# Key, query and value casts spread over three engines in a routed attention and gated FFN kernel, with a new order of all work

## The chip, the cores and the metric

The kernel runs on one core of one Trainium2 chip. The metric is device time in microseconds (us) of one execution. Three executions of the kernel before are shown; their median is 237.74 us.

## The reference, cut to what matters

Attention with 4 batches, 8 heads, 768 tokens and 64 values a head: each query and key is assigned to one of 16 centroids of its head, and a query attends only to keys of its own cluster. The result is the input of a feed-forward block with a short convolution as gate.

```python
q_assign = argmax(einsum('bhsd,hcd->bhsc', q_n, c_n))      # k_assign alike
mask = q_assign[..., :, None] == k_assign[..., None, :]
scores = where(mask, scale * q @ k.T, -1e9)
x = softmax(scores) @ v                                     # heads side by side: 512 columns
h = maximum(x @ w_in, 0)                                    # 512 -> 1024
conv_out = sum(conv_w[i] * shifted(h, i - 1) for i in 0..2) # along the sequence
out = (h * sigmoid(conv_out)) @ w_out                       # 1024 -> 512
```

## The kernel before, in words

**Pairs.** The 32 heads are worked in 16 pairs (0 to 15), four to a batch. A pair's queries and keys are loaded as f32, turned so that the head dimension lies on the partitions (tile `qkT`, 128 rows: head one on rows 0 to 63, head two on 64 to 127), and assigned to clusters. For the scores they are needed as f16 in a tile `ext` of 67 rows a head: 64 rows of values and three rows that carry the cluster number as a large negative bias. There are five `ext` tiles, used in turn (pair g has number g mod 5), and five f16 value tiles.

**Casts.** All casts end in `copy` (L317 to L321), which by a letter takes ScalarE (`a`, L319), VectorE (`d`, L321) or GpSimd (`p`, L321 as well). There are four ways to fill `ext`: `cast_by_head` (L327, token `CD`: 64 x 768, pair 0), `cast_half` (L334, `CE`: one head, queries or keys, half of the tokens, 64 x 384, straight to its place; eight of them to a pair), and `cast_pair` (L330, `CC`: both heads together, 128 x 384, four to a pair), after which head two lies on rows 64 to 127 and `shift_pair` (L338, `CX`) moves it to rows 0 to 63 of its own place by a DMA of 192 KB on SyncE's queue. `cast_v` (L342, `CV`) casts the values of one head, 128 x 384.

**Attention.** A batch has eight attention steps: per pair the first 512 queries, then the other 256. `scores` (L452, `S`) makes the score products into PSUM on TensorE, `exps` (L466, `E`) takes 1024 exponentials a row on ScalarE (144 such instructions), `values` (L476, `V`) multiplies with the values, `reciprocals` (L493, `P`) and `normalize` (L497, `N`) finish on VectorE.

**Assignment.** `assign` (L345, `A`) multiplies with the centroids, and seven steps of `argmax` (L373, `M0` to `M6`) find the cluster on VectorE, the last two on either VectorE or GpSimd.

**FFN.** Once a batch's attention is done its FFN runs between the attention steps of the next: `ffn_in` (L545, `I`), `relu` (L560, `Ra` on ScalarE or `Rd` on VectorE), `tap` (L590, tokens `a`, `b`, `c`) and `add_side` (L595, `s`, `u`) for the convolution on VectorE, `tanh` (L613, `H`, ScalarE), `gate` (L623, `G`, VectorE), `ffn_out` (L638, `O`), `evac` (L653, `Fd` or `Fa`) and the store. For the last units the convolution runs on TensorE with diagonal matrices (`conv`, L600, `W`), which the set-up makes from the weights (24 instructions, L779, `_tpd` on VectorE or `_tp` on GpSimd).

**Order.** Nothing reorders the program. A string `PLAN` (L26 on) of about 1,700 tokens is walked by L882, and each token issues one step. Each engine runs its own instructions in that order, and waits for the others by semaphores. The letter in a cast's token names its engine.

Of the kernel before, what the change touches and what calls it, by code (L numbers as in the profile page):

```python
# [26 lines left out]
    "_cent LQ.0.0 _hz.1 _zero _pk.2 _cT _k.0@0 _v.2 _n0 _pk.3 LK.0.0 _k.1@0 _id _k.2@0 _cw0 _v.0 _k.3@0 _io "  # L27
    "_id16 _pk.1 _k.4@0 LV.0 _n1 _k.5@0 _v.3 _hz.2 _pk.0 LK.0.1 _k.6@0 _nq _v.1 _v.4 _k.7@0 _hz.0 _n8 _n2 "
    "LQ.0.1 _k.8@0 _k.9@0 LQ.1.0 _k.10@0 _n3@1 _cw1@2 LK.1.0 _k.11@0 _n4 T.0.0@3 _n6 _n7 LK.1.1 T.0.1@0 _n5 "
    "_cw2 Qa.0.0 _tpd.0 _kk.0@1 _tp.1 _kk.1@2 Qd.0.1 LV.1 CVa.0.1 _kk.2@3 _kk.3@1 _kk.4@2 _tpd.2 CVa.0.0 "  # L30
    "A.0.0@0 _tpd.3 _tpd.4 LQ.1.1 CDa.0.0.0 _tpd.5 _kk.5@2 _tpd.6 _kk.6@1 CDp.0.0.1 M0.0.0 _kk.7@3 M1.0.0 "
    "T.0.2@3 M2.0.0 T.0.3@0 LV.2 Qa.0.2 M3.0.0 _tpd.7 M4.0.0 Qa.0.3 LQ.2.0 M5.0.0 M6.0.0 CDa.0.1.0 A.0.1@0 "
    "_tpd.8 _tpd.9 _tp.10 KB.0.0.1@3 M0.0.1 KB.0.0.0@1 CDp.0.1.1 BBa.0.0.1.0 M1.0.1 LK.2.0 T.1.2@0 "
    "BBd.0.0.0.0 BBd.0.0.0.1 S.0.0@0 M2.0.1 LQ.2.1 BBd.0.0.1.1 CVa.1.0 CVp.1.1 S.0.1@1 "
    "E.0.0@0 M3.0.1 LK.2.1 M4.0.1 T.1.0@3 M5.0.1 E.0.1@1 M6.0.1 T.1.1@1 LQ.3.0 _tp.11 Qd.1.0 S.0.2@0 Qd.1.2 "
    "LK.3.0 V.0.0@2 CVa.2.1 CEp.1.0.0.0 V.0.1@2 Qa.1.1 KB.0.1.0@3 CEd.1.0.1.1 KB.0.1.1@0 E.0.2@0 LQ.3.1 "
    "_tpd.12 CEp.1.1.1.0 BBd.0.1.0.1 A.1@1 BBd.0.1.0.0 CEp.1.1.1.1 BBd.0.1.1.0 LK.3.1 CEa.1.0.1.0 BBd.0.1.1.1 "
    "V.0.2@2 CEp.1.1.0.0 CEa.1.1.0.1 S.0.3@1 M0.1 LQ.4.0 CEa.1.0.0.1 S.0.4@0 M1.1 E.0.3@1 T.2.0@1 P.0.0 M2.1 "
    "T.2.1@0 _tpd.13 Qa.2.0 M3.1 T.2.2@3 E.0.4@0 M4.1 LQ.4.1 CEp.2.0.0.0 S.0.5@1 M5.1 CEp.2.1.0.0 V.0.3@1 "
    "Qd.2.2 Qa.2.1 LK.4.1 S.4.0@0 M6.1 _tpd.14 CEa.2.1.1.1 CEp.2.0.1.1 K.1@3 A.2@0 Ba.1 CEd.2.1.0.1 CVa.2.0 "  # L40
    "BX.1 N.0.0 T.3.0@3 E.0.5@1 CEp.2.0.0.1 M0.2 V.0.4@1 LQ.5.0 CEp.2.1.1.0 T.3.2@2 Qd.3.0 "
    "E.4.0@0 CEp.2.0.1.0 V.0.5@1 LQ.5.1 M1.2 T.3.1@0 CCp.3.0.0 P.0.1 LQ.6.0 S.4.1@1 Qa.3.2 N.0.1 S.4.2@0 M2.2 "
    "E.4.1@1 LK.4.0 X.0@2 Qd.3.1 CCp.3.1.1 V.4.0@1 T.4.0@3 E.4.2@0 M3.2 LK.5.1 A.3@0 CCp.3.1.0 M4.2 CCp.3.0.1 "
    "LK.5.0 Qa.4.0 M5.2 S.1.0@1 M6p.2 M0.3 Ya.0 S.1.1@0 CCp.4.0.0 M1.3 "
    "E.1.0@1 K.2@0 V.4.1@1 V.4.2@1 Bd.2 M2.3 BX.2 T.5.0@0 E.1.1@0 P.4.0 N.4.0 S.1.2@1 CX.3 _tp.15 Qd.5.0 "
    "V.1.0@1 E.1.2@1 S.1.3@0 LW.0 M3.3 CCp.5.0.0 V.1.1@1 M4.3 X.4@0 T.4.2@2 E.1.3@0 _tpd.16 M5p.3 LV.3 "
    "V.1.2@1 _tp.17 Qd.4.2 S.1.4@1 Ya.4 S.1.5@0 P.1.0 E.1.4@1 CCp.4.1.1 T.4.1@2 LV.4 N.1.0 T.5.2@0 M6p.3 "
    "E.1.5@0 Qd.4.1 S.2.0@1 Qd.5.2 K.3@1 T.5.1@3 CCp.4.0.1 "
    "E.2.0@1 S.2.1@0 Bd.3 _tpd.18 BX.3 _tpd.19 A.4@1 _tpd.20 _tpd.21 E.2.1@0 _tpd.22 _tpd.23 CCp.5.1.1 LW.1 "
    "S.2.2@1 M0.4 Qa.5.1 CCp.4.1.0 V.1.3@0 LW.2 S.2.3@0 M1.4 E.2.2@1 CCp.5.1.0 A.5@3 CWd.0 E.2.3@0 LW.3 "  # L50
    "S.2.4@1 M2.4 V.1.4@0 CVp.3.0 V.1.5@0 E.2.4@1 M0.5 S.2.5@0 CCp.5.0.1 LW.4 M1.5 V.2.0@1 CVp.4.0 E.2.5@0 "
    "V.2.1@1 P.1.1 V.2.2@1 M3.4 S.3.0@1 CVp.4.1 P.2.0 M4.4 V.2.3@3 LW.5 "
    "E.3.0@1 S.3.1@0 N.2.0 M2.5 V.2.4@3 V.2.5@3 E.3.1@0 N.1.1 S.3.2@1 M3.5 LW.6 P.2.1 M5p.4 V.3.0@0 M4.5 "
    "X.1@1 CWp.1 E.3.2@1 S.3.3@0 M5.5 Yd.1 V.3.1@0 E.3.3@0 M6.5 M6.4 S.3.4@1 N.2.1 CWp.2 V.3.2@0 K.5@3 "
    "E.3.4@1 X.2@1 LW.7 Bd.5 S.3.5@0 Yd.2 K.4@3 CVp.3.1 P.3.0 E.3.5@0 Bd.4 S.5.0@1 CWd.3 V.3.3@3 LQ.7.0 "
    "V.3.4@3 N.3.0 "
    "E.5.0@1 S.5.1@0 CWd.4 V.3.5@3 E.5.1@0 S.5.2@1 P.3.1 LQ.6.1 N.3.1 V.5.0@0 X.3@3 E.5.2@1 S.6.0@0 LK.6.1 "
    "Yd.3 V.5.1@0 I.0.1@3 "
    "E.6.0@0 LK.6.0 CWd.6 I.0.0@1 CWa.5 LQ.7.1 Rd.0.1 I.1.1@2 CX.4 Ra.0.0 CWa.7 b.0.0 I.1.0@1 LK.7.1 b.0.1 "
    "c.0.0 Ra.1.1 c.0.1 V.5.2@0 a.0.0 S.6.1@1 Ra.1.0 a.0.1 I.2.1@2 P.5.0 C.0 s.0 E.6.1@1 C.1 LZ.8.0.0 S.6.2@0 "  # L60
    "u.0 Ra.2.1 I.2.0@1 a.1.0 LZ.8.0.1 H.0 a.1.1 b.1.0 I.3.0@2 b.1.1 LZ.8.0.2 c.1.0 E.6.2@0 G.0 LK.7.0 "
    "T.6.0@3 S.7.0@1 Ra.2.0 BX.4 S.7.1@0 c.1.1 Qa.6.0 C.2 I.3.1@1 s.1 Ra.3.0 LZ.8.0.3 "
# [851 lines left out]
```

## Time and profile before

| | |
|---|---|
| median of three executions | 237.74 us (237.20 to 237.86) |
| profiled execution | 237.67 us, of it span 235.9 us, 1.8 us around it |
| granted TensorE clock | 1.00 throughout |
| TensorE, busy | 224.7 us (95%) |
| VectorE, busy | 217.1 us (92%), 565 instructions |
| ScalarE, busy | 207.5 us (88%), 273 instructions |
| GpSimd, busy | 72.3 us (31%), 166 instructions |
| DMA engines, share of the span | 65% in SyncE's queue |

Busy time counts from an instruction's start to its end, overlaps once. An instruction's end overlaps the start of the next on its engine by some 0.07 us, so the distance from start to start, which the timeline shows, is a bit less than the mean duration in the groups. A matmul's end is modelled, so that a busy TensorE may still have gaps. In the groups of instructions L321 holds VectorE's and GpSimd's copies and casts alike; the engine and the tile tell them apart.

### The profile page before, as it was taken

The page shows a single profiled execution, that of the slowest core. Times are in us where ns is not written, and L with a number is a line of the kernel's source. Part 1 is how long each engine was busy: PE and PEld are TensorE (multiplying, and loading weights), DVE is VectorE, ACT ScalarE, POOL GpSimd, SP SyncE. Part 2 cuts the span into 40 slices and gives each one's busy share as a digit, 9 for nine tenths or more (in the row PEclk, how much of TensorE's full clock was granted, in tenths as well). Part 3 has the DMA queues.
Part 4 walks back from the last instruction along what each step waited for, and adds up shares of the span by engine and source line. Part 5 has one row for each costly group of instructions (what it writes and reads, how often), then busy time and mean ns, then how long its engine had stood idle before and what let it go on. Part 6 is the DMA issues. An engine that isn't in the chain of part 4 may idle for free.

```text
span 235.9 us, 6248 instructions
## 1 busy us (share of the span) xinstructions
PE 224.7 (95%) x2345; PEld 143.7 (61%) x2345; DVE 217.1 (92%) x565; ACT 207.5 (88%) x273; POOL 72.3 (31%) x166
## 2 busy tenths in 40 slices
PE   7698999899999999999999999999999999999984
PEld 3365775666757555665466768755666766676741
DVE  4899999969999999999999999999999999999942
ACT  5688999999999999998999999998899899994531
POOL 3554756501672241476230312356010000200000
PEclk9999999999999999999999999999999999999999
DMA  6999888999794599995944989355410411033024
GB/s 154 252 249 190 177 244 312 375 208 149 146 195 42 123 126 198 137 230 87 201 84 98 187 181 194 64 162 174 134 24 3 137 50 23 3 99 134 15 93 174
DMA packets 94343, 34.35 MB, mean 146 GB/s; under 512 B 84753, under 2 KB 88873, under 8 KB 94313
## 3 DMA queue, kind: packets, MB, share of 16 engines
q1 hardware_dynamic: 94169, 33.92, 65.0%
q8 instruction: 18, 0.29, 0.6%
q14 instruction: 12, 0.10, 0.2%
q10 hardware_dynamic: 144, 0.03, 0.1%
HBM read 23.11 MB, written 6.29 MB: 125 GB/s over the span
## 4 chain that ended last, share of the span: by engine, by line
PE 69%; DVE 20%; ACT 4%; issue 2%; DMA 1%; SPq 0%; DVEq 0%
PE sc L457 19%; PE flex L551 16%; PE flex L484 11%; PE flex L641 11%; PE sc L641 4%; PE flex L354 3%; ACT attn L471 3%; PE flex L306 3%; DVE taps L779 2%; DVE eqq L389 2%; DVE sim L380 2%; DVE cnv L598 2%; DVE qkT L321 2%; DVE qkT L315 1%; DVE x L507 1%
## 5 line engine op out<-in xcount | busy, mean ns | idle before, releaser
L471 ACT ACTIVATE attn<-sc 128x1024 f16<-128x1024 f32 x144 | 140.9, 1044 | 4.5 <-PE sc L457 3.9
L457 PE MATMUL sc<-ext 67*128 67x256 f16 (+1 forms) x384 | 81.7, 326 | 1.0 <-DVE ext L321 0.4
L484 PEld LDWEIGHTS <-attn 128*128 128x128 f16 x1152 | 46.5, 97 | 17.3 <-issue 3.7
L484 PE MATMUL flex<-v,attn 128*128 128x65 f16 x1152 | 50.3, 193 | 0.4 <-DVE x L507 0.4
L457 PEld LDWEIGHTS <-ext 67*128 67x128 f16 x384 | 37.8, 112 | 19.8 <-issue 5.7
L321 POOL CAST ext<-qkT 128x384 f16<-128x384 f32 (+2 forms) x64 | 36.8, 592 | 37.5 <-PE sc L457 13.3
L551 PE MATMUL flex<-xT,w_in 128*128 128x512 f16 (+1 forms) x248 | 45.9, 327 | 0.0
L641 PE MATMUL flex<-w_out,hg 128*128 128x512 f16 x152 | 40.5, 379 | 0.0
L593 DVE TENSOR_SCALAR side<-hpad,cwcol 128x510 f16<-128x510 f16 (+1 forms) x112 | 34.1, 346 | 1.1 <-ACT hpad L565 0.8
L551 PEld LDWEIGHTS <-w_in 128*128 128x128 f16 x256 | 24.4, 97 | 15.6 <-issue 0.8
L598 DVE TENSOR_TENSOR cnv<-cnv,side 128x1020 f16<-128x1020 f16 (+1 forms) x44 | 30.8, 700 | 0.5
L629 DVE SCALAR_TENSOR_TENSOR hg<-th,hpad 128x1020 f16<-128x1020 f32 (+2 forms) x30 | 29.6, 1006 | 0.2
L574 POOL COPY hf<-hpad 128x6 f16<-128x6 f16 x16 | 6.4, 399 | 71.6 <-ACT hpad L565 37.6
L641 PEld LDWEIGHTS <-hg 128*128 128x128 f16 x192 | 17.6, 97 | 17.1 <-issue 1.2
L621 ACT ACTIVATE th<-cnv 128x1020 f32<-128x1020 f16 (+1 forms) x22 | 23.6, 1082 | 0.8 <-DVE cnv L598 0.6
L321 POOL CAST v<-v_in 128x384 f16<-128x384 f32 x27 | 16.4, 621 | 20.6 <-DMA v_in<-in_v_dram 12.7
L565 ACT ACTIVATE hpad<-flex 128x512 f16<-128x512 f32 x35 | 20.7, 609 | 2.3 <-PE flex L551 2.1
L507 DVE TENSOR_TENSOR x<-flex,rec 128x256 f16<-128x256 f32 x48 | 19.5, 416 | 0.7
L593 DVE TENSOR_SCALAR cnv<-hpad,cwcol 128x510 f16<-128x510 f16 (+1 forms) x56 | 17.3, 336 | 0.0
L315 DVE STREAM_TRANSPOSE qkT<-qk_in 128x384 f32<-128x384 f32 x32 | 16.7, 551 | 0.0
L306 PE MATMUL flex<-id,qk_in 128*128 128x128 f32 x96 | 14.0, 277 | 0.9 <-DMA qk_in<-in_q_dram 0.7
L354 PE MATMUL flex<-qkT,cP 128*32 128x384 f32 x120 | 13.0, 498 | 0.3 <-DVE x L507 0.3
(89 smaller groups left out, 205.5 us busy)
## 6 DMA issues: line engine op xcount, KB each, us to landing
v_in<-in_v_dram SPq DMA_DIRECT2D x16, 384.0 KB
out_dram<-o_sb SPq DMA_DIRECT2D x24, 256.0 KB
qk_in<-in_q_dram SPq DMA_DIRECT2D x16, 192.0 KB
qk_in<-in_k_dram SPq DMA_DIRECT2D x16, 192.0 KB
qk_in<-in_q_dram SPq DMA_DIRECT2D x32, 96.0 KB
qk_in<-in_k_dram SPq DMA_DIRECT2D x32, 96.0 KB
ext<-ext SPq DMA_DIRECT2D x13, 192.0 KB
hg<-in_moe_w_in_dram SPq DMA_DIRECT2D x4, 512.0 KB
```

Source lines behind the costliest of these rows:

```text
L306: nc.tensor.transpose(bank[at][:, P * i : P * (i + 1)], blocks, id128[:])
L321: (nc.vector if name == "d" else nc.gpsimd).tensor_copy(out=to, in_=src)
L457: nc.tensor.matmul(to[:, m], lhsT=keys[:, kt], rhs=ext_b[g % NE][0:KR, h, 0, Q0[a] : Q0[a] + QN[a]], start=True, stop=True, skip_group_che ...
L471: nc.scalar.activation(to, sc[at].rearrange("p n s -> p (n s)"), AF.Exp, scale=0.125)
L484: nc.tensor.matmul(avp(at)[:, jq + (2 * h if a else 0), 0 : D + 1], lhsT=attn[t, i // 3][:, o : o + P], rhs=v16_b[g % NE][:, h, kt, 0 : D ...
L507: nc.vector.tensor_tensor(out=to, in0=src, in1=by, op=ALU.mult)
L551: nc.tensor.matmul(bank[at][:, QN[a] * f : QN[a] * (f + 1)], lhsT=w_in16[:, r, f0 + (a + 1) * p + f, :], rhs=xT[:, b % 2, r, Q0[a] : Q0[a] ...
L593: nc.vector.tensor_scalar(out=products(n, i)[:, f], in0=src, scalar1=w, scalar2=None, op0=ALU.mult)
L598: nc.vector.tensor_tensor(out=cnv, in0=cnv, in1=side, op=ALU.add)
L621: nc.scalar.activation(to, pre, AF.Tanh, scale=0.5)
L629: nc.vector.scalar_tensor_tensor(out=hg_b[b][:, f0 + fs.start : f0 + fs.stop, LO[a] : LO[a] + N], in0=rows_of(th_t[n], n)[:, fs], scalar=1 ...
L641: nc.tensor.matmul(bank[at][:, 0:Dm], lhsT=hg_b[b][:, fb, P * tq : P * (tq + 1)], rhs=w_out16[:, fb, :], start=(fb == 0), stop=(fb == NFB ...
```

## The change

Only `PLAN` is another. Line numbers of functions grow by 4, since the string is four lines longer. What it holds differs in three ways.

**Engines.** The instructions of each kind are the same in number but for the casts below; they go to other engines:

| | VectorE | ScalarE | GpSimd |
|---|---|---|---|
| casts 128 x 384 into `ext` | 0 -> 10 | 0 -> 8 | 52 -> 22 |
| casts 64 x 384 into `ext` | 2 -> 23 | 4 -> 4 | 10 -> 13 |
| casts 64 x 768 into `ext` | 0 -> 1 | 2 -> 3 | 2 -> 0 |
| casts of values | 0 -> 4 | 5 -> 9 | 27 -> 19 |
| casts of weights, 1024 a row | 4 -> 3 | 2 -> 1 | 2 -> 4 |
| relu, 512 a row | 12 -> 19 | 36 -> 29 | |
| diagonal matrices for the convolution | 19 -> 24 | | 5 -> 0 |

VectorE loses one copy each of `qkT` with 512 and with 384 columns, one of `xT` and two of bias rows to ScalarE, and takes over one of the small `spk` copies and one step each of the last two of `argmax`.

**Way of the fourth to sixth pair** (3, 4, 5). They were cast by four `CC` each and shifted by `CX`; now by eight `CE` each and without a shift. SyncE's queue has ten shifts instead of thirteen. Of the 24 casts VectorE has 16 and GpSimd 8.

**Order.** All steps stand in a new order. One line of the string before and the line of now with the same pairs:

```diff
-    "E.4.1@1 LK.4.0 X.0@2 Qd.3.1 CCp.3.1.1 V.4.0@1 T.4.0@3 E.4.2@0 M3.2 LK.5.1 A.3@0 CCp.3.1.0 M4.2 CCp.3.0.1 "
...
-    "E.1.0@1 K.2@0 V.4.1@1 V.4.2@1 Bd.2 M2.3 BX.2 T.5.0@0 E.1.1@0 P.4.0 N.4.0 S.1.2@1 CX.3 _tp.15 Qd.5.0 "
+    "LK.5.1 CEd.3.1.1.0 E.4.2@0 CEd.3.0.1.1 LQ.6.0 S.1.0@1 M3.2 T.4.0@3 CEd.3.0.1.0 "
```

**Place one: the fourth pair's casts.** On GpSimd before, from the second pair's casts (`ext_90`) to those of the fourth (`ext_92`) and the fifth (`ext_93`):

```order
L321 CAST ext_90<-qkT 64x384 x4
L321 CAST ext_91<-qkT 64x384 x6
L321 CAST ext_92<-qkT 128x384 x4
L411 TENSOR_TENSOR pack_101<-pack_101 128x2x2x6
L321 CAST ext_93<-qkT 128x384
```

Now GpSimd has two of the fourth pair's eight, and the rest stand on VectorE between the attention of the first and fifth step (`x`, `rec`) and the third pair's argmax (`eqq`, `val`, `best`):

```order
L325 CAST ext_92<-qkT 64x384
L325 COPY xT<-flex_71 128x512
L325 CAST ext_92<-qkT 64x384 x2
L397 TENSOR_TENSOR val<-eqq,iota_78 128x384
L325 CAST ext_92<-qkT 64x384
L400 TENSOR_REDUCE best<-val 128x24
L325 CAST ext_92<-qkT 64x384
L384 STREAM_TRANSPOSE sim<-flex_68 128x384
```

VectorE's row before at this place, with the argmax of the third pair:

```order
L380 STREAM_TRANSPOSE sim<-flex_68 128x384
L321 COPY qkT<-flex_71 128x512
L384 TENSOR_REDUCE mx<-sim 128x24
L495 RECIPROCAL rec<-flex_69 128x4
L507 TENSOR_TENSOR x_437<-flex_69,rec 128x4x64
L389 TENSOR_TENSOR eqq<-sim,mx 128x384
```

Casts now stand between the steps of the argmax, where there were none but those of GpSimd beside it.

**Place two: the middle of the kernel, with the eleventh to thirteenth pairs** (`ext_89` is pair 10, `ext_91` pair 12) and the first batch's FFN (`side`, `cnv`). VectorE before:

```order
L629 SCALAR_TENSOR_TENSOR hg<-th,hpad_1_104 128x2x510
L593 TENSOR_SCALAR cnv<-hpad_0_103,cwcol 128x510
L567 TENSOR_SCALAR hpad_1_104<-flex_70 128x512
L598 TENSOR_TENSOR cnv<-cnv,side_2131 128x1020
L315 STREAM_TRANSPOSE qkT<-qk_in 128x384 x2
L593 TENSOR_SCALAR side_2191<-hpad_0_103,cwcol 128x510
```

VectorE now:

```order
L511 TENSOR_TENSOR x_2021<-flex_71,rec 128x2x2x64
L597 TENSOR_SCALAR side_1937<-hpad_1_104,cwcol 128x510
L597 TENSOR_SCALAR side_2029<-hpad_1_104,cwcol 128x510 x2
L325 CAST ext_89<-qkT 128x384
L602 TENSOR_TENSOR cnv<-cnv,side_2029 128x1020
L319 STREAM_TRANSPOSE qkT<-qk_in 128x384 x2
L499 RECIPROCAL rec<-flex_70 128x4
L602 TENSOR_TENSOR cnv<-cnv,side_1937 128x1020
L511 TENSOR_TENSOR x_2089<-flex_70,rec 128x2x2x64
L319 STREAM_TRANSPOSE qkT<-qk_in 128x384
L325 CAST ext_91<-qkT 128x384
```

The casts of these pairs were GpSimd's alone; now some stand in VectorE's row between the convolution's products and sums.

285 rows, old and new, of the table PLAN are left out of this document.

## The prediction

> **What bounds the kernel now.** I read the page first: how busy the engines are, and where the chain that ended last ran.
>
> ```profile
> span 235.9 us, 6248 instructions
> PE 224.7 (95%) x2345; PEld 143.7 (61%) x2345; DVE 217.1 (92%) x565; ACT 207.5 (88%) x273; POOL 72.3 (31%) x166
> PE 69%; DVE 20%; ACT 4%; issue 2%; DMA 1%; SPq 0%; DVEq 0%
> ```
>
> TensorE holds the chain for 69%, VectorE for 20%, and GpSimd does not appear in it. An average over stages says little, so next came the busy time by stretches (columns: stretch, length, then TensorE, its weight loads, VectorE, ScalarE and GpSimd, busy us with counts).
>
> ```profile
> 0.00:10.00 10.00, 7.05 (x42) 3.87 (x42) 6.15 (x27) 6.09 (x11) 4.08 (x31) 1.00 0.84 183
> 10.00:50.00 40.00, 37.15 (x464) 25.10 (x465) 37.12 (x101) 37.01 (x50) 20.45 (x37) 1.00 0.98 256
> 50.00:100.00 50.00, 48.84 (x524) 30.48 (x523) 47.91 (x128) 49.34 (x66) 18.74 (x35) 1.00 0.90 145
> 100.00:180.00 80.00, 79.97 (x864) 50.84 (x861) 78.78 (x198) 76.59 (x98) 27.48 (x57) 1.00 0.62 135
> 180.00:220.00 40.00, 40.00 (x399) 27.41 (x397) 39.15 (x102) 33.88 (x43) 1.58 (x6) 1.00 0.21 68
> 220.00:236.00 16.00, 11.66 (x65) 6.05 (x62) 8.00 (x15) 4.59 (x11) 0.00 (x0) 1.00 0.26 98
> ```
>
> From 100 us to 180 us TensorE is busy for 79.97 of 80 and VectorE for 78.78. Both are full, and that is the row that matters. VectorE's whole idle time is 235.9 - 217.1 = 18.8 us: 3.85 in the first 10 us, 2.88, 2.09, 1.22 and 0.85 in the four stretches behind, and 7.9 in the tail. Between 10 and 220 us, where nearly all of the moved work lies, only 7.0 us of VectorE are free. The granted clock is 1.00 in every row, so nothing is to be had there. Last came the waits: does anyone wait for a cast on GpSimd, or for a shift?
>
> ```profile
> POOL ext L321 <- PE sc L457: 13.3, 4, 7.5
> PEld L457 <- DVE ext L321: 0.7, 1, 0.7
> PEld L457 <- POOL ext L321: 0.3, 1, 0.3
> SPq L424 <- DMA ext<-ext: 3.9, 6, 0.9
> ```
>
> The columns are total us, times, longest. The scores wait 0.3 us for GpSimd's casts in the whole run; GpSimd itself waits 13.3 us for its `ext` tiles to come free. A shift is waited for only by SyncE's queue, 3.9 us over six times, and no engine waits behind it. So a quicker cast and three shifts fewer are worth at most these 0.3 us to TensorE: I count both at nothing, since GpSimd runs ahead of its readers. If that lead were gone, a shift would cost about the 0.9 us of the longest such wait.
>
> **What the change does to VectorE.** The prices, as groups by shape (columns: count, busy us, mean ns of one; then idle time ahead of it):
>
> ```profile
> L321 DVE CAST ext<-qkT 64x384 f16<-64x384 f32 x2 | 0.9, 458 | 0.0
> L567 DVE TENSOR_SCALAR hpad<-flex 128x512 f16<-128x512 f32 x12 | 8.2, 686 | 0.6 <-PE flex L551 0.5
> L321 DVE COPY qkT<-flex 128x512 f32<-128x512 f32 x10 | 6.7, 686 | 0.7 <-PE flex L306 0.4 <-issue 0.2
> L779 DVE TENSOR_SCALAR taps<-id,cwcol 128x128 f16<-128x128 f16 x19 | 5.3, 321 | 0.0
> ```
>
> Only two casts of 384 elements ran on VectorE before, so I looked at both in the timeline (start, us):
>
> ```profile
> 16.17 0.35 DVE L321 CAST ext<-qkT 64x384 f16<-64x384 f32 x1
> 16.45 0.50 DVE L779 TENSOR_SCALAR taps<-id,cwcol 128x128 f16<-128x128 f16 x1
> ...
> 22.40 0.57 DVE L321 CAST ext<-qkT 64x384 f16<-64x384 f32 x1
> 22.98 0.42 DVE L507 TENSOR_TENSOR x<-flex,rec 128x256 f16<-128x256 f32 x1
> ```
>
> From start to start one took 0.28 us, the other 0.58 us; GpSimd cast at the time of the second (below it is shown that this matters). VectorE gets 10 casts of 128 x 384, 21 of 64 x 384 and 4 of values, all of 384 elements a row: 35 x 0.30 = 10.5 us, with bounds 9.8 and 20.3. I take 0.30, close to the free one, since GpSimd will cast less. One of 768 elements: 0.5 us, under two of the free ones. Seven relus at 686 ns less some 0.07 us of overlap: 7 x 0.62 = 4.3 us. Five diagonal matrices at 321 ns less the overlap: 5 x 0.25 = 1.2 us. Six copies and casts leave, none longer than the 686 ns of the `qkT` copy, and three small steps come: between 0 and -3.7 us, taken as -2.0. Sum: 10.5 + 0.5 + 4.3 + 1.2 - 2.0 = +14.5 us, twice what is free between 10 and 220 us.
>
> **What GpSimd's lighter load gives back.** VectorE's instructions that read and write SBUF alone take longer while GpSimd casts. Four products of one shape ran mostly ahead of five casts of GpSimd, and four more beside them:
>
> ```profile
> 148.62 0.86 DVE L593 TENSOR_SCALAR side<-hpad,cwcol 128x258 f16<-128x258 f16 x4
> ...
> 149.94 1.86 DVE L593 TENSOR_SCALAR side<-hpad,cwcol 128x258 f16<-128x258 f16 x4
> ```
>
> ```profile
> 149.40 0.51 POOL L321 CAST v<-v_in 128x384 f16<-128x384 f32 x1 [3.46 <-PE flex L484]
> 149.86 1.41 POOL L321 CAST ext<-qkT 128x384 f16<-128x384 f32 x3
> 151.21 0.51 POOL L321 CAST v<-v_in 128x384 f16<-128x384 f32 x1
> ```
>
> The second four took 1.0 us longer beside 2.3 us of GpSimd's work: 0.43 us lost for each of its us, and that is the worst place. The average is lower. The same groups over the whole run, and from 180 to 220 us, where GpSimd is idle:
>
> ```profile
> L593 DVE TENSOR_SCALAR side<-hpad,cwcol 128x510 f16<-128x510 f16 x64 | 21.0, 363 | 1.1 <-ACT hpad L565 0.8
> L593 DVE TENSOR_SCALAR side<-hpad,cwcol 128x258 f16<-128x258 f16 x48 | 13.1, 324 | 0.0
> L598 DVE TENSOR_TENSOR cnv<-cnv,side 128x1020 f16<-128x1020 f16 x32 | 22.6, 707 | 0.3
> ```
>
> ```profile
> L598 DVE TENSOR_TENSOR cnv<-cnv,side 128x1020 f16<-128x1020 f16 x10 | 6.9, 685 | 0.1
> L593 DVE TENSOR_SCALAR side<-hpad,cwcol 128x510 f16<-128x510 f16 x20 | 6.2, 350 | 0.1
> L593 DVE TENSOR_SCALAR side<-hpad,cwcol 128x258 f16<-128x258 f16 x16 | 3.8, 284 | 0.0
> ```
>
> 13 ns x 64, 40 ns x 48 and 22 ns x 32 make 0.8 + 1.9 + 0.7 = 3.4 us lost in these three groups. They are a quarter of VectorE's time (56.7 of 217.1 us); the products into `cnv`, the diagonal matrices and the small argmax steps lose as well, others (those that read PSUM) hardly, so I estimate 6 to 10 us in all for 72 us of GpSimd, about 0.11 for each us. GpSimd's own relief:
>
> ```profile
> L321 POOL CAST ext<-qkT 128x384 f16<-128x384 f32 x52 | 30.1, 597 | 29.8 <-PE sc L457 13.3 <-DVE qkT L315 7.8 <-ACT qkT L319 4.1
> L321 POOL CAST v<-v_in 128x384 f16<-128x384 f32 x27 | 16.4, 621 | 20.6 <-DMA v_in<-in_v_dram 12.7 <-PE sc L457 4.3 <-PE flex L484 3.5
> L779 POOL TENSOR_SCALAR taps<-id,cwcol 128x128 f16<-128x128 f16 x5 | 3.3, 668 | 3.5 <-DVE cwcol L773 3.3
> L321 POOL CAST w_in<-hg 128x1024 f16<-128x1024 f32 x2 | 2.4, 1209 | 0.1
> ```
>
> 30 x 0.597 + 8 x 0.621 + 5 x 0.668 - 2 x 1.209 = 23.8 us less; the other shapes about cancel. At 0.11 that gives VectorE 2.6 us, at the worst place's 0.43 it would give 10.2. I take 3.0. Net for VectorE: 217.1 + 14.5 - 3.0 = 228.6 us busy.
>
> Here the Trainium skill can be weighed. "SBUF — State Buffer" (Who interferes with whom) says that VectorE in its two-port modes and GpSimd exclude each other for a whole instruction, and the later one stands still. Taken at its word for every cast removed, the 23.8 us would come back nearly whole; the rows above show a part of that, since many of VectorE's instructions are not of that kind and many casts fall between them. [...]
>
> **ScalarE and the queue.** ScalarE gets eight casts of 384, four of values, one of 768 and a few copies, and loses seven relus and a weight cast:
>
> ```profile
> L565 ACT ACTIVATE hpad<-flex 128x512 f16<-128x512 f32 x35 | 20.7, 609 | 2.3 <-PE flex L551 2.1 <-issue 0.2
> L319 ACT ACTIVATE ext<-qkT 64x384 f16<-64x384 f32 x4 | 2.1, 522 | 0.6 <-DVE qkT L321 0.6
> ```
>
> Twelve times 0.522 less seven times 0.609 is +2.0 us, with the others perhaps +4. It has 3.4 us free between 100 and 180 us and 28.4 us in all, so I count it at nothing; were its cover gone, 2 us would show.
>
> **The sum.** VectorE's time is its work and what it must stand idle. The tail's 7.9 us stay, since the last gates come before the last products. Of the first 10 us I leave 2.5 idle, because diagonal matrices now stand there earlier. In the 210 us between I leave 1%, 2.1 us, a bit under the 1.5% of its fullest stretch. 228.6 + 7.9 + 2.5 + 2.1 = 241.1 us. An engine with a backlog starts its instructions closer together, for which I take off 1.5 us (an estimate: 0.19 us from start to start in the free four above against 0.25 for the mean of 324 ns less the overlap). The span is then 239.6 us; with the 1.8 us around it 241.4 us. This stands against the profiled execution's 237.67 us, which lies 0.07 us under the median. With the bounds: 0.43 in place of 0.11 for half of the casts, and a backlog worth 3 us, give 238.6; casts at 0.43 us give 246.
>
> **Rivals and chances.** A measurement of this kernel tells no less than about 0.3%, 0.7 us, from no change: 237.0 to 238.4 is "the same".
> - VectorE becomes the bound, as summed: 241.4 us, by itself 238.6 to 246. For it speaks the row of 78.78 us in 80. Chance 0.60.
> - Faster, one mechanism: GpSimd's casts cost VectorE more than the average says, because they fall beside the convolution's products as at 149.9 us. At 0.43 the relief is 10.2 us, VectorE gains only 14.5 - 10.2 = 4.3 us, which fits into the 5.0 us that are free between 10 and 100 us, and TensorE decides again. TensorE stands idle for 2.85 us between 10 and 50 us and 1.16 us between 50 and 100 us; with the casts spread, half of that goes, 2.0 us: 235.7 us. It decides from a relief of about 8 us on. Against it: the three groups' means. Chance 0.23. The rule of "SBUF — State Buffer" is what this rival would follow.
> - The load fits: a relief of 7 us leaves +7.5 us, the 7.0 us that are free between 10 and 220 us swallow it, and nothing else changes: 237.7 us. Chance 0.13.
> - Worse: VectorE's casts meet GpSimd's as the second one at 22.40 us did, 0.58 us each: 35 x 0.28 = 9.8 us more work, half of it in stretches that have no room: 246.3 us. Chance 0.04.
>
> Range: 235.6 to 246.0. Faster 0.23, same 0.14 (0.13 and the edge of the first case), slower 0.63.
>
> **What would show it.** Right: VectorE over 98% busy from 50 to 180 us, its total near 227 to 230 us, GpSimd near 48 us, the `side` products of 258 columns near 300 ns, and TensorE with gaps in the middle that end with VectorE. The sum is wrong if VectorE's busy time stays under 222 us: then the relief was mis-sized. It is wrong in another way if VectorE is as busy as I say and the span still stays under 237 us: then its idle time was not needed.

## The result, and the profile after

| | before | after |
|---|---|---|
| median, measured together (four executions each) | 237.53 us (237.20 to 237.86) | 241.13 us (240.92 to 241.91) |
| ratio | | 1.015 (95% interval 1.0128 to 1.0172) |
| profiled execution; its span | 237.67; 235.9 us | 240.97; 238.8 us |

The change makes the kernel 1.5% slower. The forecast of 241.4 us is 0.3 us off, but the sum behind it is not what happened. From the page of the changed kernel, its span, its busy times and its chain:

```profile
span 238.8 us, 6239 instructions
PE 225.3 (94%) x2345; PEld 142.7 (60%) x2345; DVE 220.2 (92%) x610; ACT 211.2 (88%) x282; POOL 49.5 (21%) x124
PE 61%; DVE 27%; ACT 7%; issue 2%; DMA 1%; DVEq 0%; ACTq 0%
```

VectorE works 3.1 us more than before, not 11.5. The stretches of the changed kernel, with the same columns as before (after TensorE and its weight loads, the third pair of numbers is VectorE):

```profile
0.00:10.00 10.00, 7.45 (x50) 3.99 (x50) 7.63 (x38) 6.53 (x13) 2.00 (x28) 1.00 0.85 185
10.00:50.00 40.00, 37.20 (x451) 24.50 (x448) 38.60 (x110) 37.43 (x49) 15.02 (x27) 1.00 0.94 248
50.00:100.00 50.00, 48.83 (x534) 30.14 (x532) 49.65 (x138) 49.13 (x66) 11.90 (x25) 1.00 0.97 163
100.00:180.00 80.00, 80.00 (x877) 51.74 (x874) 79.75 (x221) 78.94 (x105) 18.05 (x38) 1.00 0.59 114
180.00:220.00 40.00, 39.76 (x379) 25.78 (x377) 38.93 (x98) 31.19 (x38) 2.57 (x6) 1.00 0.25 77
220.00:239.00 19.00, 12.11 (x68) 6.53 (x68) 5.66 (x11) 8.01 (x17) 0.00 (x0) 1.00 0.22 83
```

From 50 to 180 us VectorE is busy for 129.4 of 130 us, as I said it would be. But TensorE beside it does as much as before: 128.83 us in the same stretch, against 48.84 + 79.97 = 128.81. VectorE filled up, and TensorE did no less beside it. VectorE's share of the chain did grow, from 20% to 27%, so that the chain alone does not clear it; e11 and e12 below do. Up to 180 us the two kernels are level, and the last row holds the difference. From 220 us on before needed 15.9 us for 11.66 us of TensorE's work; now it needs 18.8 us for 12.11.

The same can be seen in the progress of the work. The table gives the start of the last exponential of an attention step, and of the first input product of the last FFN group (I.22), in us:

| | first batch (E.7.2) | third batch, first half (E.19.5) | last step (E.31.2) | I.22 starts | end | from I.22 to the end |
|---|---|---|---|---|---|---|
| before | 63.0 | 142.2 | 211.3 | 216.0 | 235.9 | 19.8 |
| after | 62.5 | 142.2 | 208.6 | 217.0 | 238.8 | 21.9 |

The attention ends 2.7 us earlier, yet the last FFN group starts 1.0 us later and what follows takes 2.1 us more. Behind the last exponential and ahead of I.22 now stand eleven output products, where there were seven, and most of unit 20, over half of which ran between attention steps before; unit 21 stood mostly behind them in both.

The groups of the changed kernel that answer to my prices (count, busy us, mean ns):

```profile
L602 DVE TENSOR_TENSOR cnv<-cnv,side 128x1020 f16<-128x1020 f16 x32 | 22.0, 687 | 0.1
L597 DVE TENSOR_SCALAR side<-hpad,cwcol 128x510 f16<-128x510 f16 x64 | 19.9, 343 | 0.0
L325 POOL CAST ext<-qkT 128x384 f16<-128x384 f32 x22 | 14.0, 656 | 38.3 <-DVE rec L499 15.2 <-PE sc L461 10.9 <-DVE qkT L319 10.4
L571 DVE TENSOR_SCALAR hpad<-flex 128x512 f16<-128x512 f32 x18 | 12.3, 681 | 0.3 <-PE flex L555 0.2
L597 DVE TENSOR_SCALAR side<-hpad,cwcol 128x258 f16<-128x258 f16 x48 | 11.8, 284 | 0.1
L325 POOL CAST v<-v_in 128x384 f16<-128x384 f32 x19 | 9.8, 531 | 27.5 <-DMA v_in<-in_v_dram 15.9 <-PE flex L645 5.4 <-PE flex L488 4.3
L325 DVE CAST ext<-qkT 64x384 f16<-64x384 f32 x23 | 8.6, 380 | 0.4
L783 DVE TENSOR_SCALAR taps<-id,cwcol 128x128 f16<-128x128 f16 x24 | 4.7, 246 | 0.1
L325 DVE CAST ext<-qkT 128x384 f16<-128x384 f32 x10 | 3.4, 341 | 0.0
```

The added casts cost what I took: 341 to 380 ns less 0.07 us of overlap is 0.27 to 0.31 us. But most of what else on VectorE touches SBUF alone is now faster: the products of 258 columns take 284 ns, which before was so only where GpSimd stood idle, and the diagonal matrices 246 ns in place of 321. I compared every VectorE instruction of a shape that ran beside GpSimd with those of the same shape that ran alone: the excess over the whole run is 9.8 us before and 3.1 us after. It depends on how one counts (mean or median of those alone, any overlap or more than half of the length): 8.7 to 10.7 us before and 2.9 to 4.4 us after.

### The profile page after: what moved, and what is told of

It reads as the page before. It is cut to its first block, busy times and chain, and to the rows that moved or that the text cites. A ratio compares the mean times of both kernels' runs of the same rounds, so it can differ in the third digit from the quotient of the medians.

```text
span 238.8 us, 6239 instructions
## 1 busy us (share of the span) xinstructions
PE 225.3 (94%) x2345; PEld 142.7 (60%) x2345; DVE 220.2 (92%) x610; ACT 211.2 (88%) x282; POOL 49.5 (21%) x124
## 4 chain that ended last, share of the span: by engine, by line
PE 61%; DVE 27%; ACT 7%; issue 2%; DMA 1%; DVEq 0%; ACTq 0%
PE sc L461 17%; PE flex L555 12%; PE flex L645 11%; PE flex L488 10%; ACT attn L475 4%; PE sc L645 4%; DVE ext L325 3%; PE flex L358 2%; DVE qkT L325 2%; DVE x L511 2%; DVE side L597 2%; DVE cnv L602 2%; PE sc L555 2%; DVE taps L783 2%; DVE sim L384 2%
## 5 line engine op out<-in xcount | busy, mean ns | idle before, releaser
L461 PE MATMUL sc<-ext 67*128 67x256 f16 (+1 forms) x384 | 83.1, 327 | 0.7 <-ACT attn L475 0.3
L488 PE MATMUL flex<-v,attn 128*128 128x65 f16 x1152 | 51.3, 193 | 0.2
L461 PEld LDWEIGHTS <-ext 67*128 67x128 f16 x384 | 36.7, 112 | 16.9 <-issue 5.8
L555 PE MATMUL flex<-xT,w_in 128*128 128x512 f16 (+1 forms) x224 | 43.3, 329 | 0.0
L645 PE MATMUL flex<-w_out,hg 128*128 128x512 f16 x152 | 40.6, 379 | 0.3 <-DVE hg L633 0.3
L555 PEld LDWEIGHTS <-w_in 128*128 128x128 f16 x256 | 24.4, 97 | 14.2 <-issue 0.2
L597 DVE TENSOR_SCALAR side<-hpad,cwcol 128x510 f16<-128x510 f16 (+1 forms) x112 | 31.7, 317 | 0.1
L325 POOL CAST ext<-qkT 128x384 f16<-128x384 f32 (+1 forms) x35 | 21.0, 615 | 49.9 <-DVE rec L499 15.2
L645 PEld LDWEIGHTS <-hg 128*128 128x128 f16 x192 | 17.4, 97 | 19.1 <-issue 3.4
L625 ACT ACTIVATE th<-cnv 128x1020 f32<-128x1020 f16 (+1 forms) x22 | 23.8, 1080 | 1.9 <-DVE cnv L602 1.6
L511 DVE TENSOR_TENSOR x<-flex,rec 128x256 f16<-128x256 f32 x48 | 19.7, 411 | 0.2
L578 POOL COPY hf<-hpad 128x6 f16<-128x6 f16 x16 | 5.3, 331 | 61.0 <-ACT hpad L569 22.7
L569 ACT ACTIVATE hpad<-flex 128x512 f16<-128x512 f32 x25 | 15.7, 631 | 0.5 <-PE flex L555 0.4
L325 POOL CAST v<-v_in 128x384 f16<-128x384 f32 x19 | 9.8, 531 | 27.5 <-DMA v_in<-in_v_dram 15.9
L310 PEld LDWEIGHTS flex<-id,qk_in 128*128 128x128 f32 x96 | 10.6, 141 | 5.0 <-issue 1.7
```

The lines of the kernel that those rows point to most:

```text
L310: nc.tensor.transpose(bank[at][:, P * i : P * (i + 1)], blocks, id128[:])
L325: (nc.vector if name == "d" else nc.gpsimd).tensor_copy(out=to, in_=src)
L461: nc.tensor.matmul(to[:, m], lhsT=keys[:, kt], rhs=ext_b[g % NE][0:KR, h, 0, Q0[a] : Q0[a] + QN[a]], start=True, stop=True, skip_group_che ...
L488: nc.tensor.matmul(avp(at)[:, jq + (2 * h if a else 0), 0 : D + 1], lhsT=attn[t, i // 3][:, o : o + P], rhs=v16_b[g % NE][:, h, kt, 0 : D ...
L511: nc.vector.tensor_tensor(out=to, in0=src, in1=by, op=ALU.mult)
L555: nc.tensor.matmul(bank[at][:, QN[a] * f : QN[a] * (f + 1)], lhsT=w_in16[:, r, f0 + (a + 1) * p + f, :], rhs=xT[:, b % 2, r, Q0[a] : Q0[a] ...
```

## The experiments

In the steps below the number behind the point names unit and part, and the one behind @ the PSUM bank; Rd and Ra are relus on VectorE and ScalarE. The line numbers of the experiments' profiles are smaller than those of the changed kernel by 25 or 27. The diffs show some of the changed steps; others, and the steps between them, are left out.

**Which part of the kernel loses the time?** First the kernels were cut at I.22: the changed order up to there and the old one behind it, and the other way round.

```diff
 e1, changed kernel, at the cut
-I.22.1@3 c.21.1 H.20 b.21.0 b.21.1 a.21.0 I.22.0@6 a.21.1 Ra.22.1 G.20 I.23.0@7
+H.20 I.22.1@7 a.21.0 b.21.0 b.21.1 c.21.1 I.22.0@6 Rd.22.1 G.20 I.23.1@3
 e2, kernel before, at the cut
-I.22.1@2 a.21.0 Fa.2.4 b.21.0 b.21.1 c.21.1 FX.2.4 I.22.0@6 C.23 Rd.22.1 G.20 I.23.1@3
+Fd.2.4 O.3.0.0@1 FX.2.4 O.3.0.1@1 C.23 O.3.1.1@7 I.22.1@3 c.21.1 b.21.0 b.21.1 a.21.0 I.22.0@6 a.21.1 Ra.22.1 G.20 I.23.0@4
```

> The changed kernel as it is up to the FFN product I.22.1 (217.0 us in its trace), and from there the remaining steps in the order, PSUM banks and engines that the kernel before has for them. Theory VectorE-load (the 3.6 us come from VectorE being full from 10 to 180 us, as the prediction summed): nothing of that is touched, so 241.1 us, at least 240.5. Rival tail (TensorE stands idle some 3.3 us longer in the last 22 us, 21.9 us for 13.9 us of products against 19.9 us for 15.2 us before, because of how the last FFN steps are ordered): 241.1 - 3.3 = 237.8 us, between 237.2 and 238.6.

Measured: 239.52 us, ratio 1.0087 (1.0060 to 1.0114). The old tail gives 1.6 of the 3.6 us back, which lies between the two forecasts. (Its banks had to be numbered anew as well, and I.22.1 and I.22.0 came to lie in one tile, see e11; what this cost it was not separated.)

> The reverse: the kernel before up to I.22.1 (216.0 us in its trace), from there the remaining steps in the order, banks and engines of the changed kernel. VectorE-load: as before, 237.5 us, at most 238.3. Tail: 237.5 + 3.3 = 240.8 us, between 239.8 and 241.5.

Measured: 237.54 us, ratio 1.0008 (0.9983 to 1.0032). The new tail behind the old beginning costs nothing, as the load theory had it: from I.22 to the end it takes 18.5 us, where nearly the same order takes 21.9 us in the changed kernel. I read this at first as a matter of what had been done ahead of the cut. There was another difference, which I had made myself: to join the pieces, other steps than in the changed kernel had to take banks 4 and 7. It became clear only with e11.

**Is it the engines, or the order?** e3 puts the new engines of casts, diagonal matrices and relus (and the way of pairs 3 to 5) into the old order. e4 gives the casts alone back to their old engines in the new order; pairs 3 to 5 stay head by head, so that GpSimd has all of their 24 casts.

```diff
 e3, kernel before
-CCp.3.0.0 CX.3
+CEp.3.0.0.0 CEd.3.0.1.0
 e4, changed kernel
-CEd.1.0.0.0 CCd.15.0.1 CVa.14.0
+CEp.1.0.0.0 CCp.15.0.1 CVp.14.0
```

> The kernel before in its own order, but every cast, every diagonal matrix and every relu ahead of I.22.1 on the engine that the changed kernel gives it, and pairs 3 to 5 cast head by head without a shift. VectorE gets the full extra work (about 14 us of instructions), the tail stays. VectorE-load: 241 to 243 us, since an order that was not made for these engines does not use them better. Tail: the load is paid for by what GpSimd gives back; 237.5 to 239 us, VectorE's busy time near 220 us.

Measured: 259.6 us, ratio 1.0942 (1.0898 to 1.0987), far above both forecasts. From the page of e3 and its row from 10 to 50 us:

```profile
PE 232.3 (90%) x2345; PEld 144.9 (56%) x2345; DVE 231.5 (90%) x614; ACT 209.5 (82%) x276; POOL 49.4 (19%) x126
DVE 40%; PE 30%; ACT 14%; issue 7%; SPq 3%; DMA 3%; POOL 1%; DVEq 0%; ACTq 0%; POOLq 0%
```

```profile
10.00:50.00 40.00, 31.91 (x363) 19.72 (x363) 38.85 (x107) 32.06 (x42) 11.89 (x24) 1.00 0.81 207
```

Here is what I had forecast for the change: VectorE works 231.5 us, holds 40% of the chain, and TensorE goes short, 31.91 us of work in the second stretch in place of 37.15. The first batch's attention ends at 75.5 us instead of 63.0. (From 50 to 100 us the granted clock is 0.93 in e3, so that not all of the 22 us need be VectorE's own.) VectorE's slowdown beside GpSimd is 8.1 us (8.0 to 9.3 in the other ways of counting), though GpSimd works as little as in the changed kernel (49.4 us against 49.5, with 3.1 us): what counts is which instructions stand beside its casts.

> The changed kernel in its own order with the casts on the engines that they had before (pairs 3 to 5 still head by head, on GpSimd, 24 casts). VectorE loses about 11 us of cast instructions and gets the disturbance by GpSimd back. VectorE-load: faster than the changed kernel, 238 to 239.5 us. Tail: the tail is the same, so 241 us or, where a cast on GpSimd comes late, up to 243 us.

Measured: 245.57 us, ratio 1.0341 (1.0299 to 1.0383), 4.4 us slower than the changed kernel, and above both forecasts. Its row from 10 to 50 us:

```profile
10.00:50.00 40.00, 35.86 (x413) 23.65 (x414) 30.22 (x82) 35.37 (x48) 24.21 (x46) 0.96 0.86 228
```

GpSimd now works 24.21 us there, VectorE 30.22, and E.7.2 comes at 66.6 us, 4.1 us later than in the changed kernel. From there to E.31.2 it takes 146.6 us, the changed kernel 146.1. So casting on three engines is worth 4 us at the beginning, in an order made for it, and nothing behind it. The comparison flatters it: the 24 casts of 64 x 384 cost GpSimd 13.3 us in e4 (556 ns each), where the twelve of 128 x 384 that the kernel before has for these pairs cost 7.2 us (597 ns each). The old way of pairs 3 to 5, with its shifts, was not run in the new order.

> The kernel before, its order unchanged, with only the casts of pairs 6 to 15 (key casts and value casts, 26 steps in all) on the engines that the changed kernel gives them; pairs 3 to 5, the diagonal matrices and the relus stay as before. The same order with all engines of the changed kernel took 259.6 us, 22 us over the kernel before. If the loss comes from the head (pairs 3 to 5, diagonal matrices), this one takes 238 to 242 us and the end of E.7.2 stays near 63.0 us. If each cast that stands in VectorE's queue at a place made for GpSimd holds up what is behind it, wherever it is, it takes 245 to 252 us, and the time is lost evenly between 63 and 200 us.

```diff
 e9, kernel before: 26 steps of pairs 6 to 15
-CCp.6.0.0 CCp.8.0.0 CVp.15.0
+CCa.6.0.0 CCd.8.0.0 CVa.15.0
```

Measured: 240.54 us, ratio 1.0144 (1.0117 to 1.0170). The middle casts alone cost the old order some 3 us, as the first forecast had it. In the profiled execution, the slowest of the four (242.03 us), E.7.2 comes at 64.7 us, 1.7 us late, E.19.5 at 145.8 us, 3.6 late, and E.31.2 at 215.4 us, 4.1 late. So most of e3's 22 us belong to pairs 3 to 5, the earliest casts, the diagonal matrices and the relus. Which of these it is was not separated.

**Does VectorE's load matter in the new order?** e5 gives the 26 middle casts back to GpSimd, e7 moves four relus ahead of the last group from VectorE to ScalarE.

```diff
 e5, changed kernel
-CCa.6.0.0 CCd.8.0.0 CVa.14.0
+CCp.6.0.0 CCp.8.0.0 CVp.14.0
 e7, changed kernel
-Rd.19.0 Rd.19.1 Rd.20.0 Rd.20.1
+Ra.19.0 Ra.19.1 Ra.20.0 Ra.20.1
```

> The changed kernel in its own order, with the casts of pairs 6 to 15 alone (pair and value casts, 10 + 4 on VectorE, 8 and some on ScalarE) back on GpSimd; the first six pairs keep their engines. VectorE-load: the casts in the full middle are what costs, so the last exponential comes about 2 to 3 us earlier than in the changed kernel and the time falls to 238.5 us. Tail: VectorE's casts in the middle cost nothing net, since GpSimd disturbs again: 241 us within 0.7, and the stretch from the end of step 7 (62.5 us) to the last exponential (208.6 us) stays at 146 us.

Measured: 240.75 us, ratio 1.0155 (1.0109 to 1.0200). The row of e5 from 100 to 180 us:

```profile
100.00:180.00 80.00, 79.80 (x868) 51.62 (x867) 79.36 (x211) 75.68 (x95) 26.74 (x55) 1.00 0.57 113
```

GpSimd works 8.7 us more there than in the changed kernel and VectorE 0.4 us less. The time stays. This shows that the engine of these casts is indifferent here, and not yet that VectorE's load is: VectorE stays full, and over the whole run it works 218.9 us instead of 220.2, though 14 casts left it.

> The changed kernel with the four relus of units 19 and 20 (197 to 211 us) on ScalarE instead of VectorE, 2.5 us less for VectorE right ahead of the tail. If VectorE's backlog there is what delays the normalisation at 215.4 us and with it the last FFN group: I.22 comes about 2 us earlier and the time falls to 239 to 239.8 us. If the order of the tail itself sets it: 240.6 to 241.4 us, or slower where the exponentials have to wait for ScalarE.

Measured: 240.51 us, ratio 1.0137 (1.0106 to 1.0169). VectorE works 216.9 us, less than in the kernel before, and the interval still overlaps that of the changed kernel. This speaks against the load of VectorE as the cause, but only for the end of the run, where the four relus stand. What settles it are e11 and e12.

**Does the start of the last group set the end?** e6 brings I.22 and I.23 forward, ahead of the convolution of units 20 and 21. e8 and e10 leave the convolution's order alone and put output products behind the group, where TensorE waits, instead of ahead of it: six in the changed kernel, three in e2. e8 also brings the normalisation of the second to last attention step (N.30, X.30, Ya.30) forward and puts I.22.0 into bank 5.

```diff
 e6, changed kernel: the last group ahead of units 20 and 21
-Fd.2.3 O.3.1.0@4 Ra.21.1 O.3.2.0@1 s.20 FX.2.3 O.3.0.0@0 C.21 N.30.0
+I.22.1@3 Ra.21.0 c.20.0 c.20.1 I.22.0@5 Ra.21.1 Fd.2.3 FX.2.3 I.23.0@7 Ra.22.1 s.20 C.21
 e8, changed kernel: output products behind the group
-Fd.2.3 O.3.1.0@4 Ra.21.1 O.3.2.0@1 s.20 FX.2.3 O.3.0.0@0 C.21 N.30.0
+Fd.2.3 I.22.1@3 Ra.21.1 s.20 FX.2.3 I.22.0@5 C.21 FX.2.4 O.3.1.0@4 C.23 FX.2.5 b.20.1 O.3.2.0@1
 e10, e2 with three output products behind the group
-Fd.2.4 O.3.0.0@1 FX.2.4 O.3.0.1@1 C.23 O.3.1.1@7 I.22.1@3
+Fd.2.4 FX.2.4 C.23 I.22.1@3
```

> The changed kernel up to the reciprocal P.30.0, then the same steps on nearly the same engines with the last attention step's normalisation, its transposes and the FFN products of units 22 and 23 ahead of the convolution work of unit 20, and the last products of the output behind. VectorE-load: the same work is only moved, VectorE and TensorE are full up to 217 us, so nothing is won: 240.5 to 241.5 us. Tail: the last FFN group starts at about 213.5 instead of 217.0 us and the chain behind it keeps its length, so the end comes 2 to 3 us earlier: 238 to 239.2 us.

Measured: 244.7 us, ratio 1.0304 (1.0269 to 1.0339), a miss. I.22 starts at 214.1 us, 2.9 us earlier, and the end comes 3.5 us later. Two waits of e6 from 214 us on (total us, times, longest):

```profile
DVE hg L608 <- ACT th L600: 5.3, 2, 4.6
PE flex L620 <- DVE hg L608: 2.8, 2, 2.5
```

VectorE stands 4.6 us at a gate of the last group, with the convolution of units 20 and 21 queued behind it; then TensorE waits 2.5 us for the gate of unit 21. A step brought forward in a queue makes what it passes late when it has to wait itself. Why it waits so long has to do with the banks, which e11 below explains. The gate waits for the tanh of W.22.2, which lies in bank 6:

```profile
218.05 0.49 PE L583 MATMUL sc<-hpad,taps 128*128 128x258 f16 x3
...
220.34 0.49 PE L583 MATMUL sc<-hpad,taps 128*128 128x258 f16 x3
...
220.93 0.39 ACT L600 ACTIVATE th<-sc 128x258 f32<-128x258 f32 x1 [2.52 <-PE sc L583]
```

The first line is W.22.2, done at 218.54 us. The tanh starts 2.4 us later, right behind W.22.1, the second line, which goes into bank 7. So over half of the 4.6 us comes from the choice of banks; how e6 would end without it was not run.

> The changed kernel, the same work, with six 0.43 us output products of the last 128 rows (O.3.1.0, O.3.2.0, O.3.0.0, O.3.0.1, O.3.1.1, O.3.2.1) taken from ahead of the last FFN group's input products and put between and behind them; the multiplication of the second to last item (N.30) stands right behind its reciprocal; the order of convolution and gates on VectorE is kept. Theory A (the chain from the last group's input products to the output bounds the end, and the changed order puts output products ahead of it that could fill TensorE's waits behind it): the group starts 1 to 2 us earlier than the 217.0 us of the changed kernel, what follows stays at 21 to 22 us, and the time is 239.0 to 240.3 us; ratio to the kernel before 1.006 to 1.011. Theory B (TensorE's total work alone sets the end, the place of the products is indifferent): 241 us, ratio 1.014 to 1.016. Theory C (convolution and gates on VectorE set the end, as when the group was brought forward by 2.9 us): what follows grows by what the start gains, 241 to 243 us.

Measured: 239.26 us, ratio 1.0083 (1.0066 to 1.0101). I.22 starts at 214.3 us, 2.7 us earlier, and the rest grows from 21.9 to 23.2 us. Half of the start's gain arrives: the time is that of theory A, but what follows I.22 grows, as theory C had it, though by less.

> The kernel before up to the last FFN group, then the changed kernel's order, but with the three output products O.3.0.0, O.3.0.1 and O.3.1.1 (0.43 us each) behind the group's input products instead of ahead of them. With them ahead it took 237.54 us (group at 217.4 us, 18.5 us behind it). Theory A (the chain behind the group sets the end): the group starts near 216.1 us, 18.5 to 19.3 us follow, 236.2 to 237.0 us, ratio 0.995 to 0.998. Theory B (TensorE's total sets the end): 237.5 us, ratio 1.000.

Measured: 237.34 us, ratio 1.0000 (0.9979 to 1.0021). I.22 starts at 215.6 us (e2: 217.4), the rest takes 19.7 us (18.5). My 236.2 to 237.0 was missed; the gain is too small to tell from none. With nearly the same order behind I.22, e2 and e10 take 18.5 and 19.7 us, the changed kernel and e8 21.9 and 23.2: some 3.4 us that neither load nor order explains.

**Which step waits for what?** That left the banks. TensorE's results lie in eight PSUM banks; in the code four of them are tiles of their own and the other four the halves of two tiles:

```python
sc = [psum.tile([P, 2, 512], F32, name=f"sc{i}") for i in range(2)]
flex = [psum.tile([P, 512], F32, name=f"flex{i}") for i in range(4)]
bank = [x[:] for x in flex] + [sc[i // 2][:, i % 2, :] for i in range(4)]
```

So banks 4 and 5 are one tile, 6 and 7 another. The timeline of the changed kernel (start us, length us, and in brackets the idle time before and what ended it), where the halves of the last group come out of TensorE:

```profile
217.85 1.91 PE L555 MATMUL sc<-xT,w_in 128*128 128x256 f16 x16
217.85 1.63 PEld L555 LDWEIGHTS <-w_in 128*128 128x128 f16 x15
218.05 0.60 ACT L569 ACTIVATE hpad<-flex 128x512 f16<-128x512 f32 x1
...
219.80 0.60 ACT L569 ACTIVATE hpad<-sc 128x512 f16<-128x512 f32 x1 [1.15 <-PE sc L555]
220.45 0.78 PEld L608 LDWEIGHTS <-taps 128*128 128x128 f16 x8 [0.97 <-ACT hpad L569]
```

The 16 products are eight of I.22.0 into bank 6 and eight of I.23.0 into bank 7. The relu of bank 6 could start after the first eight, near 218.9 us. It starts at 219.80 us, when the last of the 16 is done. A later relu, of I.23.1 in bank 5, from the timeline at 224 us:

```profile
224.33 1.04 PE L555 MATMUL sc<-xT,w_in 128*128 128x256 f16 x8
...
225.20 0.59 PE L645 MATMUL sc<-w_out,hg 128*128 128x512 f16 x2
...
225.84 0.60 ACT L569 ACTIVATE hpad<-sc 128x512 f16<-128x512 f32 x1 [2.02 <-PE sc L645]
```

Its own products end at 225.37 us; it is released by an output product, L645, which goes into bank 4 and which it does not read. And at the very end, where output products alternate between banks 6 and 7:

```profile
230.22 1.03 PE L645 MATMUL sc<-w_out,hg 128*128 128x512 f16 x4
...
231.28 0.60 ACT L662 ACTIVATE o_sb<-sc 128x512 f32<-128x512 f32 x1 [1.56 <-PE sc L645]
...
231.93 1.02 PE L645 MATMUL sc<-w_out,hg 128*128 128x512 f16 x4 [0.69 <-ACT o_sb L662]
...
232.99 0.60 ACT L662 ACTIVATE o_sb<-sc 128x512 f32<-128x512 f32 x1 [1.11 <-PE sc L645]
233.64 1.46 PE L645 MATMUL sc<-w_out,hg 128*128 128x512 f16 x6 [0.69 <-ACT o_sb L662]
```

Twice TensorE waits for 0.69 us until ScalarE has copied a bank out, and the next product in its order goes into the other half (O.3.3.3 into bank 6 behind the copy of 7, O.3.4.1 into 7 behind the copy of 6). e11 changes not one step of the order, only 13 bank numbers, of which four are shown:

```diff
 e11, changed kernel: banks 4 and 7 swapped from O.3.1.0 on
-O.3.1.0@4 I.23.0@7 O.3.5.0@7 O.3.4.0@7
+O.3.1.0@7 I.23.0@4 O.3.5.0@4 O.3.4.0@4
```

> The changed kernel with not one step moved: only PSUM banks 4 and 7 are swapped from O.3.1.0 on (13 steps: O.3.1, O.3.4, O.3.5 and I.23.0). Banks 4 and 5 are the halves of one tile in the code, 6 and 7 of another. Theory A (a step that reads one half waits for a write to the other half that stands ahead of it, since the wait is by tile): in the changed kernel the relu Ra.22.0 of bank 6 waits for I.23.0 into bank 7 (it starts at 219.80, right after it; 0.9 us lost), and at the end O.3.3.3 into bank 6 waits for Fa.3.5 out of bank 7 and O.3.4.1 into 7 for Fa.3.3 out of 6 (0.65 us each). With the swap these pairs lie in different tiles: 1.3 to 2.3 us less, 238.7 to 239.8 us, ratio 1.005 to 1.010, and the relu starts by 219.2. Theory B (the waits are the chain's own, banks are indifferent): 241 us, ratio 1.013 to 1.017. Theory C (too few output products left as filler): the gaps stay, 240.5 to 241 us.

Measured: 238.25 us, ratio 1.0035 (1.0003 to 1.0067); the span of the profiled execution is 235.9 us, as before the change, and from I.22 to the end it takes 18.7 us. The gain is larger than theory A had forecast (238.7 to 239.8 us), and B and C are out. The same three places in e11 (its L530, L544, L620 and L637 are L555, L569, L645 and L662 above), each from its own view:

```profile
218.05 1.91 PE L530 MATMUL sc<-xT,w_in 128*128 128x256 f16 x16
...
219.12 0.60 ACT L544 ACTIVATE hpad<-sc 128x512 f16<-128x512 f32 x1 [0.28 <-PE sc L530]
```

```profile
223.29 1.04 PE L530 MATMUL sc<-xT,w_in 128*128 128x256 f16 x8
...
224.17 0.59 PE L620 MATMUL sc<-w_out,hg 128*128 128x512 f16 x2
224.37 0.60 ACT L544 ACTIVATE hpad<-sc 128x512 f16<-128x512 f32 x1 [1.49 <-PE sc L530]
```

```profile
230.21 1.89 PE L620 MATMUL sc<-w_out,hg 128*128 128x512 f16 x8
230.41 0.60 ACT L637 ACTIVATE o_sb<-sc 128x512 f32<-128x512 f32 x1 [0.27 <-DMA out_dram<-o_sb]
```

The first relu starts while the second half of the 16 products still runs. The second one is released by its own products, and starts beside the output product that it waited for before. The last products run through beside the copy; the view shows the last eight of twenty in one stretch. In this kernel, then, a step waits for the whole tile, also for the half that it does not use. The first relu starts 0.7 us earlier than in the changed kernel, the second 1.5, and the last products end at 232.10 us instead of 235.10, which is all that the spans differ by.

e12 takes nearly the order of e8 (O.3.1.0 and O.3.2.0 change places, and I.23.1 goes ahead of W.23.1) and gives the steps of the tail banks whose other half is not in use at that time, with an exception.

```diff
 e12, e8 with other banks
-I.22.0@5 O.3.1.0@4 I.23.0@7 I.23.1@5 O.3.5.0@7 O.3.3.0@6
+I.22.0@6 O.3.1.0@2 I.23.0@4 I.23.1@7 O.3.5.0@2 O.3.3.0@0
```

> The order of e8 (output products behind the last group's input products; it took 239.26 us), with the banks chosen so that no step of the tail waits for the other half of a tile: I.22.0 in 6, I.23.0 in 4, I.23.1 in 7 and ahead of W.23.1, O.3.1 and O.3.5 in 2, O.3.3 in 0, O.3.4 in 7. Theory A (shared tiles, and fillers ahead of the group, are what the end loses): the gains of e8 (1.5 to 2 us) and of the swap of banks (1.3 to 2.3 us) add up, with one output wait of 0.65 us more gone: 236.3 to 238.0 us, ratio 0.996 to 1.003, level with the kernel before or ahead of it. Theory B (something earlier, in units 20 and 21, holds the end): 238.5 to 239.5 us, as e8.

Measured: 236.49 us, ratio 0.9964 (0.9944 to 0.9984), which is faster than both kernels. Its trace has none of the two waits of 0.69 us. The exception is the relu of I.23.1 in bank 7: its products end at 221.72 us, but it starts at 222.52 us, released by W.23.1 in bank 6, so that some 0.8 us are still lost at this place. From the page of e12:

```profile
span 233.8 us, 6240 instructions
PE 224.4 (96%) x2345; PEld 142.3 (61%) x2345; DVE 218.3 (93%) x610; ACT 210.8 (90%) x282; POOL 49.9 (21%) x124
```

VectorE works as much as in the changed kernel within 2 us, every step is on the same engine, and the kernel is 4.6 us faster than that one.

## Why the prediction was right in number and wrong in its reasons

- **"VectorE becomes the bound, as summed": failed.** The fullness was there (over 99% from 50 to 180 us, more than the 98% I named), the effect was not: TensorE did as much work in that stretch as before. e11 and e12 have every step on the engine that the change gives it, and VectorE works 218.9 and 218.3 us in them, more than the 217.1 us before the change; the times are 238.25 and 236.49 us. By the test that I had set, a total under 222 us, the sum is wrong: VectorE works 220.2 us, not 228.6.
- **The relief by GpSimd, 3.0 us: the term that was mis-sized.** It is 9.8 - 3.1 = 6.7 us (5.5 to 6.9 in the other ways of counting). I had an average price per us of GpSimd's work; but the price depends on what stands beside it. 9.8 us for 72.3 us is 0.14, 3.1 us for 49.5 us is 0.06, and e3 has 8.1 us for the same 49.4 us. The order decides it, and I had counted the order at nothing here.
- **The added work of 14.5 us: right.** The casts, at 0.27 to 0.31 us, and the relus (12.3 us for 18 against 8.2 us for 12) cost what was said. Counted from each start to the next start, or to the instruction's end where that comes first, the instructions that came to VectorE, less those that left it, cost 14.25 us, and those that both kernels have there cost 11.15 us less than before; that leaves the 3.1 us. Of the 11.15 us the relief is 6.7. For the other 4.5 I had 1.5 for closer starts; what they come from stays open. The 1.5 us were no clean term either: the mean of 324 ns, from which they were taken, holds the slowdown beside GpSimd already.
- **"The tail's 7.9 us stay": failed, and made the number come out by luck.** VectorE stands idle there for 18.8 - 5.66 = 13.1 us. The sum with what was measured is 220.2 + 13.1 + 2.4 + 3.1 = 238.8 us of span; mine was 228.6 + 7.9 + 2.5 + 2.1 - 1.5 = 239.6. Work 8.4 us too high and tail 5.2 us too low nearly cancel; the rest is 1.0 us in the middle and the 1.5 us that the measured work already holds. I took the tail's shape over from the kernel before, although the whole order was new and its rows were at hand.
- **Where the 3.6 us are:** the swap of 13 bank numbers takes the ratio from 1.0150 to 1.0035, about three quarters of the loss (by its interval, between half and nearly all). To which step the rest belongs stays open. e12 shows that a tail with other banks and output products behind the last group more than recovers what is left. What the order alone is worth there, with no shared tile, was not run by itself.
- **Casts' latency and shifts counted at nothing:** for the middle, right (e5). At the beginning the first batch's attention ends 0.5 us earlier than before, so the term is small there too. It is not nothing for the new order as such: with the casts on the old engines, and 24 of them head by head on GpSimd, it loses 4.1 us there (e4).
- **The rivals.** "The load fits", with a relief of 7 us, came nearest for the stretch up to 180 us; a rival for the tail was missing.
- **Two slips in the working.** With 0.43 for half of the 23.8 us and 0.11 for the other half the relief is 6.4 us, 3.4 more than the 3.0, and with 1.5 us more for the backlog the lower bound of the sum is 236.5 us, not 238.6. And at 149.94 us the first of the five casts is over (149.40 + 0.51), so that the second four products ran beside 1.8 us of GpSimd's work, not 2.3, and lost 0.56 us for each.

## What to carry to other kernels

When the order changes, read the stretch where nothing overlaps, the tail, step by step, and look there at which buffer each step uses: in this kernel the steps on two buffers cut from one tile wait for each other, and the sign in the trace is a wait released by an instruction that the waiting one does not read. An engine may be full without being the bound; the test is whether the engine beside it does less work in the same stretch. Engines and order belong together: the new engines cost 22 us in the old order, and in the new one the casts alone are 4 us faster on them than on the old.

## What the runs showed of the hardware

The loss that VectorE takes from GpSimd is not a rate in these runs: 8.1 us (e3) and 3.1 us (the changed kernel) for the same 49.4 and 49.5 us of GpSimd's work. GpSimd's own casts went both ways: those of values from 621 to 531 ns, those of 128 x 384 from 597 to 656 ns. A cast of 64 partitions takes VectorE no less time than one of 128 (380 and 341 ns, 384 elements a row), so casting head by head, which takes twice as many casts, about doubles the price on VectorE.
